# A DiT block: attention probabilities transposed on VectorE and by DMA instead of on TensorE

## The chip, the cores and the metric

One Trainium2 chip, one of its cores. The time is the device time of one execution in microseconds; a kernel is run several times and the median is compared. One further execution is taken with the hardware profiler, and its trace gives every instruction of the five engines: PE (TensorE), DVE (VectorE), ACT (ScalarE), POOL (GpSimd) and SP (SyncE, which here only issues DMAs).

## The reference, cut to what matters

B = 2 batches of N = 256 tokens, D = 1152, two heads of 576, F = 4608, all bf16.

```python
mod = (_silu(c) @ w_mod).reshape(B, 6, 1, D)
shift_a, scale_a, gate_a, shift_m, scale_m, gate_m = [mod[:, i] for i in range(6)]
h = _layernorm(x) * (1 + scale_a) + shift_a
q, k, v = split(h @ wqkv)                                  # 2 heads of 576
attn = _softmax(einsum('bqhd,bkhd->bhqk', q, k) * 576 ** -0.5)
a = einsum('bhqk,bkhd->bqhd', attn, v).reshape(B, N, D) @ wo
x = x + gate_a * a
h2 = _layernorm(x) * (1 + scale_m) + shift_m
return x + gate_m * (_gelu(h2 @ w_fc1) @ w_fc2)
```

## The kernel before

The 512 tokens are four tiles of 128 (t = 0 to 3; batch b holds tiles 2b and 2b + 1). The program is written as a list of units, each for one engine. A small planner (`Sched`) works out what each unit must wait for from the bytes that it reads and writes, and fixes the order on every engine before the program is emitted. TensorE and SyncE keep the order in which the units are written. VectorE, ScalarE and GpSimd are ordered by a list schedule with assumed costs. Each engine works through its order strictly, so a unit that waits holds up all units behind it on its engine. A DMA has a semaphore of its own (60 of them are reused in turn), and SyncE issues a DMA only when the buffer and the data are ready.

The stretch around the change, in the order of TensorE:

1. `q_kt*`, `proj`: the projections to q, the last with `proj(WQ, 8)`, beside which `S_b_h` computes the scores of batch b and head h (index idx = 2b + h) into one PSUM bank each (`s_bank`).
2. `s_and_softmax`: VectorE takes the row maxima (`smax`, L1005), scales them (`snb`, L1006), ScalarE takes exponentials with row sums (`sexp`, L1009), VectorE takes reciprocals (`sri`, L1011) and multiplies (`spn`, L1013). The result `PP[idx]` has queries on partitions.
3. `pt_transposes`: four 128x128 TensorE transposes for each idx (L695, helper `tr`) turn P so that keys lie on partitions; a copy (`PT_ev`) moves the result from PSUM to `PTS[idx]`, on VectorE for batch 0 and on ScalarE for batch 1.
4. `v_proj(t, ci)`: twelve tiles of nine matmuls of width 384 (L692, helper `mm`), three PSUM banks in turn, copied out by ScalarE (`v_ev`). The transposes stand between these tiles.
5. `rows`: the rows shift_m and scale_m, 9 x 2 rounds of four matmuls of width 288 that run side by side in four column strips of the array ("quads"). They stand before the last three v tiles. VectorE turns the result (`mt_0`, `mt_1`, L1050).
6. `pv_halves`, `pv`: P V, with `PTS` as the moving operand of width 256; `pv_halves` uses two column strips. VectorE and ScalarE copy the results to `OT`.
7. `wo_tile(t)`: three tiles of nine matmuls of width 384, four PSUM banks in turn (`acc`). VectorE multiplies by the gate (`wo_t1`, L1165), GpSimd adds x (`wo_x1`, L1166), then follow layernorm statistics (`bn_ln2`, `aggr`, `veps`, `rstd` on GpSimd, `nmr2`), ScalarE normalises (`xn2`, L1171), and `xn2_T(t)` transposes on TensorE. Then fc1 and fc2.

Beside this VectorE computes the attention gate gate_a (`attn_gate`: 18 steps `ga_b_kt` of 1152 elements, L1061 and L1064, then `ga_T`, `ga_red` and small ones up to `ga_t`, L1082). It is stored to a scratch tensor in HBM (`st_ga0`, `st_ga1`) and loaded back broadcast over 128 partitions as `GA[b]` (`ld_g0`, `ld_g1`). SyncE loads the weights, all in one order: after the parts of w_mod (`ld_modr`) WO, the first two quarters of WFC1 (`wfc1_load`), `GA`, two more of WFC1, `WGM`, and parts of WFC2. WO takes the bytes of the K weights, WFC1 those of the Q and V weights.

Of the kernel before, what the change touches and what calls it, by code (L numbers as in the profile page):

```python
# [9 lines left out]
SEM_LAT = 120.0  # L10
# [161 lines left out]
class Sched:  # L172
    def __init__(self):
        self.units = []
        self.instrs = []
        self.sb_recs = {}
        self.sb_buckets = defaultdict(set)
        self.bank_pe = defaultdict(list)
        self.bank_other = defaultdict(list)
        self.bank_prev_other = defaultdict(list)  # L180
        self.cur_unit = None
        self.first = {}

    def unit(self, eng, dur, name="", dma_bytes=0, boost=0.0, lat=0.0):
# [20 lines left out]

    def order_after(self, u, prev):
# [74 lines left out]
    def schedule(self, dma_bw=385.0, dma_issue=650.0, dma_lat0=900.0, dma_lat1=600.0, verbose=False):  # L281
# [30 lines left out]
        avail_time = {}  # L312
# [13 lines left out]
        while scheduled < n:  # L326
# [39 lines left out]
            for f, uid in fin_now:  # L366
                for s in units[uid].succ:
                    ndeps[s.uid] -= 1
                    at = max(avail_time.get(s.uid, 0.0), f + (SEM_LAT if True else 0.0))
# [166 lines left out]
def c_dve_tt16(n):  # L536
    return 100.0 + 1.15 * n
# [6 lines left out]
def build_kernel(nc, x, c, wqkv, wo, w_mod, w_fc1, w_fc2, out):  # L544
# [5 lines left out]
    with (  # L550
# [64 lines left out]
        PP = [sb(O_P + i * 1024, 1024).rearrange("p (j k) -> p j k", j=2) for i in range(4)]  # L615
        PTS = [sb(O_PT + i * 1024, 1024).rearrange("p (j k) -> p j k", j=2) for i in range(4)]
        GA = [sb(O_GA + b * 2304, 2304) for b in range(2)]
# [375 lines left out]
        def s_and_softmax(b, h):  # L993
# [17 lines left out]
            dve(165, lambda e: e.reciprocal(out=ri, in_=rsum), [rsum], [ri], "sri_%d" % idx)  # L1011
            rib = ri.unsqueeze(2).broadcast_to([P, 2, 256])
            u = dve(c_dve_tt16(512), lambda e: e.tensor_tensor(out=pp, in0=pp, in1=rib, op=ALU.mult), [pp, ri], [pp], "spn_%d" % idx)  # L1013
            if idx % 2 == 1:
                S.order_after(ga_units[(1, 7) if idx == 1 else (0, 8)], u)

        def pt_transposes(b, h):
            idx = b * 2 + h
            bank = s_bank[(b, h)]
            S.unit("pe", 4 * c_mm(128), "PT_%d_%d" % (b, h))  # L1020
            for kjt in range(2):
                for jq in range(2):
                    tr(ps16(bank, kjt * 256 + jq * 128, 128), PP[idx][:, jq, kjt * 128:(kjt + 1) * 128], IDENT)
            copy_on("dve" if b == 0 else "act", PTS[idx].rearrange("p j k -> p (j k)"), ps16(bank, 0, 512), 512, True, "PT_ev%d" % idx)

        v_banks = [0, 1, 2]
        v_rr = [0]

        def v_proj(t, ci):
            bank = v_banks[v_rr[0] % 3]  # L1030
# [25 lines left out]
        def attn_gate():  # L1056
# [60 lines left out]

        PVB = [(6, 7, 0, 1), (3, 4, 0, 1)]

        def pv_halves():  # L1120
            S.unit("pe", 4 * c_mm(256) + 100.0, "PV_halves")
            for b in range(2):
                for kjt in range(2):
                    for h in range(2):
                        f0 = 512 + 64 * h
                        mm(psum[64 * h:64 * h + 64, 5 * 512 + b * 256:5 * 512 + b * 256 + 256], V[:, 2 * b + kjt, f0:f0 + 64],
                           PTS[b * 2 + h][:, kjt, :], b == 0 and kjt == 0, b == 1 and kjt == 1, skip_group_check=True,
                           tile_position=(0, 64 * h))
# [219 lines left out]
```

## Time and profile before

| | |
|---|---|
| runs, not profiled | 243.26 us median of 3 (242.79 to 243.5) |
| the profiled execution | span 242.5 us from the first to the last instruction; no other time is kept of it |
| granted TensorE clock, mean | 0.993 |
| busy | PE 237.3, DVE 121.5, ACT 67.8, POOL 19.9 us |
| TensorE transposes | 89 in all, 16 of them of P |
| HBM | 50.15 MB read, 212 GB/s over the span |

The span is 0.76 us under the median of the runs. A busy share of PE counts a matmul from its start to its modelled end, and successive matmuls overlap, so the mean duration of a matmul is longer than the distance between two starts; the chain of waits, in which each matmul counts up to the next, is the better measure. The page puts the helper's line on what a helper records, so all matmuls have L692, all transposes by TensorE L695 and all DMA issues L673.

### The profile page before, as it was taken

Reading aid. Unit: us, or ns where it says so; the run is one execution under the profiler, and the core shown is the slowest. Engines: PE = TensorE matmul, PEld = TensorE weight load, DVE = VectorE, ACT = ScalarE, POOL = GpSimd, SP = SyncE. Lnnn points to the kernel's source line nnn. Section 1 sums busy time; section 2 is a strip of 40 time slices with the busy share of each in tenths; the row PEclk is TensorE's granted clock in tenths of the full one; section 3 lists DMA queues with packets and bytes.
Section 4 is the critical chain, followed back from the end, with each engine's and each line's share of the span. In section 5 each row is a group of like instructions: output and inputs, shape, how many; then the busy total and the mean of one; then the engine's idle time right before and its main releaser. Section 6 shows DMA issues by size and latency. Waiting matters only on the chain.

```text
span 242.5 us, 3957 instructions
## 1 busy us (share of the span) xinstructions
PE 237.3 (98%) x1699; PEld 145.4 (60%) x1699; DVE 121.5 (50%) x229; ACT 67.8 (28%) x136; POOL 19.9 (8%) x36
## 2 busy tenths in 40 slices
PE   6899999999999999999999999999999999999995
PEld 2688844466666666898544444444666566566564
DVE  2654379988996689669999700000022222111112
ACT  4921440435524206973233322222000000000000
POOL 1300000000002276400000110000000000000000
PEclk9979999999999999999999999999999999999999
DMA  6999999999992999999963499100000000000000
GB/s 221 378 370 392 389 392 390 398 413 402 391 352 79 312 374 391 391 348 398 352 198 83 157 313 374 43 0 3 0 16 19 16 16 16 19 16 16 21 27 20
DMA packets 30363, 51.58 MB, mean 213 GB/s; under 512 B 1547, under 2 KB 15755, under 8 KB 30347
## 3 DMA queue, kind: packets, MB, share of 16 engines
q1 hardware_dynamic: 29888, 50.73, 58.9%
q0 software_dynamic: 288, 0.60, 0.8%
q8 instruction: 13, 0.21, 0.4%
q10 hardware_dynamic: 171, 0.01, 0.0%
q14 instruction: 3, 0.02, 0.0%
HBM read 50.15 MB, written 1.19 MB: 212 GB/s over the span
## 4 chain that ended last, share of the span: by engine, by line
PE 95%; DMA 3%; SPq 1%; DVE 0%; issue 0%
PE psum L692 93%; DMA arena<-in_wqkv_dram 3%; PE psum L695 2%; SPq L673 1%; DVE arena L1290 0%; DVE arena L1291 0%
## 5 line engine op out<-in xcount | busy, mean ns | idle before, releaser
L692 PE MATMUL psum<-arena 128*128 128x384 bf16 (+8 forms) x1610 | 234.0, 314 | 2.4 <-POOL arena L718 1.5
L692 PEld LDWEIGHTS psum<-arena 128*128 128x128 bf16 (+2 forms) x1610 | 139.7, 97 | 92.4 <-issue 3.8
L1290 DVE TENSOR_TENSOR arena<-psum,arena 128x384 f32<-128x384 f32 (+2 forms) x13 | 6.8, 526 | 88.6 <-PE psum L692 88.6
L1200 ACT ACTIVATE arena<-psum 128x512 bf16<-128x512 f32 (+1 forms) x45 | 22.8, 512 | 42.1 <-PE psum L692 42.1
L687 ACT ACTIVATE arena<-psum 128x512 bf16<-128x512 f32 (+6 forms) x34 | 18.2, 560 | 37.9 <-PE psum L692 37.9
L1064 DVE SCALAR_TENSOR_TENSOR arena<-arena 128x1152 f32<-128x1152 bf16 x16 | 21.9, 1408 | 0.0
L1095 DVE SCALAR_TENSOR_TENSOR arena<-arena 128x1152 f32<-128x1152 bf16 x16 | 21.4, 1414 | 0.0
L1166 POOL TENSOR_TENSOR arena<-arena 128x384 f32<-128x384 f32 x12 | 10.9, 912 | 11.7 <-DVE arena L1165 9.5
L740 DVE BATCH_NORM_STATS2 arena<-arena 128x6 f32<-128x384 f32 (+1 forms) x18 | 9.5, 549 | 3.8 <-DMA arena<-in_x_dram 3.8
L673 POOL DMA_DIRECT2D dit_scratch<-arena x4 | 2.4, 609 | 96.6 <-DVE arena L1082 60.3
L689 DVE CAST arena<-psum 128x512 bf16<-128x512 f32 x11 | 7.2, 687 | 5.3 <-PE psum L692 5.3
L1165 DVE TENSOR_TENSOR arena<-psum,arena 128x384 f32<-128x384 f32 x12 | 6.7, 556 | 3.7 <-PE psum L692 3.7
L1171 ACT ACTIVATE arena<-arena 128x1152 bf16<-128x1152 f32 x4 | 5.4, 1344 | 9.8 <-DVE arena L1170 9.8
L695 PE MATMUL psum<-arena 128*128 128x128 bf16 (+1 forms) x89 | 7.4, 225 | 0.4 <-DMA arena<-in_c_dram 0.4
L695 PEld LDWEIGHTS psum<-arena 128*128 128x128 bf16 (+1 forms) x89 | 6.3, 102 | 2.2 <-DMA arena<-in_c_dram 1.1
L1291 DVE TENSOR_TENSOR arena<-arena 128x384 bf16<-128x384 f32 (+2 forms) x13 | 6.9, 527 | 0.5
L1190 ACT ACTIVATE arena<-psum,arena 128x128 bf16<-128x128 bf16 x16 | 6.1, 455 | 3.0 <-PE psum L695 2.2
L1187 DVE TENSOR_SCALAR arena<-psum,arena 128x128 bf16<-128x128 bf16 x20 | 5.5, 336 | 2.9 <-PE psum L695 2.9
L1009 ACT ACTIVATE arena<-psum,arena 128x256 bf16<-128x256 f32 x8 | 3.7, 471 | 0.2 <-DVE arena L1006 0.2
L744 POOL TENSOR_TENSOR arena<-arena 128x1 f32<-128x1 f32 x6 | 3.3, 555 | 4.7 <-DVE arena L743 4.5
L1005 DVE TENSOR_REDUCE arena<-psum 128x2 f32<-128x512 f32 x4 | 2.8, 688 | 0.9 <-PE psum L692 0.7
L962 ACT ACTIVATE arena<-arena 128x256 bf16<-128x256 bf16 x6 | 2.5, 495 | 1.5 <-DVE arena L956 1.5
(60 smaller groups left out, 53.9 us busy)
## 6 DMA issues: line engine op xcount, KB each, us to landing
arena<-in_w_fc_dram SPq DMA_DIRECT2D x9, 1152.0 KB, 8.0
arena<-in_w_fc_dram SPq DMA_DIRECT2D x4, 2592.0 KB, 17.6
arena<-in_wqkv_dram SPq DMA_DIRECT2D x18, 288.0 KB, 9.3
arena<-in_w_mod_dram SPq DMA_DIRECT2D x6, 864.0 KB, 12.3
arena<-in_w_mod_dram SPq DMA_DIRECT2D x3, 1728.0 KB, 20.5
arena<-in_wqkv_dram SPq DMA_DIRECT2D x1, 2592.0 KB, 17.6
arena<-in_wo_dram SPq DMA_DIRECT2D x1, 2592.0 KB, 24.9
arena<-in_w_mod_dram SPq DMA_DIRECT2D x1, 2592.0 KB, 18.5
```

The lines of the kernel that those rows point to most:

```text
L687: act(c_act(n), lambda e: e.activation(out=dst, in_=src, func=ACTF.Copy), [src], [dst], name)
L689: return dve(c_dve_psum16(n) if psum16 else c_dve_psum32(n), lambda e: e.tensor_copy(dst, src), [src], [dst], name)
L692: S.instr(lambda e: e.matmul(o, lhsT=l, rhs=r, start=st, stop=sp, **kw), reads=[l, r], writes=[o])
L695: S.instr(lambda e: e.transpose(o, i_, idn), reads=[i_, idn], writes=[o])
L740: dve(550, lambda e, s=s, o=o: e.bn_stats(out=o, in_=s), [s], [o], "bn_%s_%d" % (tag, ci))
L1064: ga_units[(b, kt)] = dve(150 + FG * 1.1, lambda e, o=o, w=w, s1=s1: e.scalar_tensor_tensor(out=o, in0=w, scalar=s1, in1=o, op0=ALU.mult, ...
L1095: u = dve(1300, lambda e, o=o, w=w, s1=s1: e.scalar_tensor_tensor(out=o, in0=w, scalar=s1, in1=o, op0=ALU.mult, op1=ALU.add), [w, s1, o], ...
L1165: dve(550, lambda e, o=o, ga=ga, x1c=x1c: e.tensor_tensor(out=x1c, in0=o, in1=ga, op=ALU.mult), [o, ga], [x1c], "wo_t1_%d_%d" % (t, ci))
L1166: S.op("pool", 930, lambda e, xs=xs, x1c=x1c: e.tensor_tensor(out=x1c, in0=x1c, in1=xs, op=ALU.add), reads=[x1c, xs], writes=[x1c], name=" ...
L1200: act(c_act(ntok), lambda e: e.activation(out=dst, in_=o, func=ACTF.Gelu_apprx_tanh), [o], [dst], "gelu_%d_%d" % (f, tok0))
L1290: dve(c_dve_psum32(w), lambda e, o=o, gm=gm, t1=t1: e.tensor_tensor(out=t1, in0=o, in1=gm, op=ALU.mult), [o, gm], [t1], "fc2_t1_%d_%d" % ( ...
L1291: dve(c_dve_32(w), lambda e, t1=t1, x1c=x1c, ost=ost: e.tensor_tensor(out=ost, in0=t1, in1=x1c, op=ALU.add), [t1, x1c], [ost], "fc2_out_%d ...
```

## The change

- The softmax keeps its exponentials in `PP[idx]`, and ScalarE scales them by the reciprocals, in two halves (`spn_idx_jq`), in place of VectorE's multiplication.
- VectorE turns P in blocks of 32x32 in one instruction for each idx (`PT_turn`), reading every fourth key column for each block and writing to the buffers that held `PTS` (now `PTF`). Four DMAs for each idx, issued by SyncE (`mv_pt`), carry rows of 1024 bytes on 32 partitions to 256 bytes on 128 partitions, back into the bytes of `PP`. `PTS[idx]` is now a view of these bytes, in which 256 query columns are eight pieces of 32. No TensorE transposes and no PSUM copies of P remain.
- `rows` moves behind the last v tile, so that `rows`, `pv_halves` and `pv` follow each other. The v tiles use four PSUM banks instead of three; `PVB` and `acc` are rearranged; `OT_ev_4` moves from VectorE to ScalarE.
- The store of the gate moves from GpSimd's queue to SyncE's (`gate_store`).
- SyncE's order becomes: w_mod parts, sixteen moves, WO, WFC1 part 0, the gate's store, `GA`, WFC1 part 1, then as before. WO was issued ahead of the softmax until now.
- `in_order` fixes the order of VectorE, ScalarE and GpSimd around these places by lists of names (without waits), and 66 DMA semaphores are in turn instead of 60.

```diff
-        dma(WO, wo_v, D * D * 2, "ld_wo", run=2304)
...
-            rib = ri.unsqueeze(2).broadcast_to([P, 2, 256])
-            u = dve(c_dve_tt16(512), lambda e: e.tensor_tensor(out=pp, in0=pp, in1=rib, op=ALU.mult), [pp, ri], [pp], "spn_%d" % idx)
...
-        def pt_transposes(b, h):
...
+            for jq in range(2):
+                o, aa = pp[:, jq, :], ri[:, jq:jq + 1]
+                act(c_act(256, 1), lambda e, o=o, aa=aa: e.activation(out=o, in_=o, func=ACTF.Copy, scale=aa), [o, aa], [o], "spn_%d_%d" % (idx, jq))
+            src, flat = pp.rearrange("p j (t x c) -> p c (j t) x", t=2, c=4), PTF[idx]
+            dve(c_dve_32(512), lambda e: e.transpose(flat, src), [src], [flat], "PT_turn%d" % idx)
+            for a in range(4):
+                dma(PPF[idx][:, 128 * a:128 * a + 128], flat[32 * a:32 * a + 32, :], P * 256, "mv_pt%d_%d" % (idx, a), run=256)
...
+        PTS = [f.rearrange("p (a j t i) -> p t j a i", a=4, j=2, t=2) for f in PPF]
...
-        v_banks = [0, 1, 2]
+        v_banks = [7, 0, 1, 2]
...
+        def gate_store():
-            dma(lin[0:64].rearrange("(j p) c -> p j c", j=2), GTA[:, 0:64].rearrange("p (j c) -> p j c", j=2), 4096, "st_ga0", eng="pool")
-            dma(lin[64:72], GTA[0:8, 64:96], 512, "st_ga1", eng="pool")
+            dma(lin[0:64].rearrange("(j p) c -> p j c", j=2), GTA[:, 0:64].rearrange("p (j c) -> p j c", j=2), 4096, "st_ga0")
+            dma(lin[64:72], GTA[0:8, 64:96], 512, "st_ga1")
...
-        PVB = [(6, 7, 0, 1), (3, 4, 0, 1)]
+        PVB = [(6, 7, 0, 1), (2, 5, 6, 7)]
...
-            S.order_after(copy_on("dve", OT[:, 4, :], ps32(5), 512, False, "OT_ev_4"), last_mt[0])
+            copy_on("act", OT[:, 4, :], ps32(5), 512, False, "OT_ev_4")
...
-        acc = [2, 3, 4, 5]
+        acc = [3, 4, 5, 2]
...
         s_and_softmax(1, 1)
-        v_proj(0, 2)
-        pt_transposes(0, 0)
-        v_proj(1, 0)
-        pt_transposes(1, 0)
-        v_proj(1, 1)
-        v_proj(1, 2)
-        pt_transposes(0, 1)
-        v_proj(2, 0)
-        v_proj(2, 1)
-        pt_transposes(1, 1)
-        v_proj(2, 2)
-        rows()
+        dma(WO, wo_v, D * D * 2, "ld_wo", run=2304)
         wfc1_load(0)
-        wfc1_load(1)
+        gate_store()
         for b in range(2):
             dma(GA[b], scratch[0, b].partition_broadcast(P), P * D * 2, "ld_g%d" % b, run=2304)
-        v_proj(3, 0)
-        v_proj(3, 1)
-        v_proj(3, 2)
+        wfc1_load(1)
+        v_proj(0, 2)
+        for t in range(1, 4):
+            for ci in range(NCH):
+                v_proj(t, ci)
+        rows()
         wfc1_load(2)
         wfc1_load(3)
...
+        ga = ["ga_%d_%d" % (b, kt) for kt in range(KT) for b in range(2)]
+        S.in_order("dve", ga)
+        S.in_order("dve", ga[9:10] + ["smax_0", "snb_0"] + ga[10:11] + ["sri_0"] + ga[11:12] + ["smax_2", "snb_2", "PT_turn0", "smax_1", "snb_1", "sri_2"]
+                   + ga[12:13] + ["smax_3", "snb_3", "sri_1", "PT_turn2"] + ga[13:14] + ["PT_turn1", "sri_3"] + ga[14:15] + ["PT_turn3"] + ga[15:16])
+        S.in_order("act", ["sexp_0_0", "sexp_0_1", "qk_ev8", "spn_0_0", "spn_0_1", "v_ev0_0", "sexp_2_0", "sexp_2_1", "sexp_1_0", "sexp_1_1", "v_ev0_1",
+                           "spn_2_0", "spn_2_1", "spn_1_0", "spn_1_1", "v_ev0_2", "sexp_3_0", "sexp_3_1", "v_ev1_0", "spn_3_0", "spn_3_1", "v_ev1_1", "v_ev1_2"])
+        S.in_order("dve", ["ga_t", "mt_0", "mt_1", "OT_ev0_2", "OT_ev0_7", "OT_ev1_2", "OT_ev1_7"])
+        S.in_order("act", ["OT_ev_4", "OT_ev0_0", "OT_ev0_5", "OT_ev1_0", "OT_ev1_5"])
...
+        S.in_order("dve", ["wo_t1_0_0", "wo_t1_0_1", "bn_ln2_0_0", "wo_t1_0_2", "bn_ln2_0_1", "wo_t1_1_0", "bn_ln2_0_2", "aggr_ln2_0", "veps_ln2_0", "wo_t1_1_1", "nmr2_0",
...
```

More of the change, by code (lines that the diff above doesn't have):

```diff
@@ L182, in __init__ @@
         self.first = {}
+        self.loose = set()
     def unit(self, eng, dur, name="", dma_bytes=0, boost=0.0, lat=0.0):
@@ L204, in instr, with in_order @@
         return ins
+    def in_order(self, eng, names):
+        by_name = {u.name: u for u in self.units if u.eng == eng}
+        for a, b in zip(names, names[1:]):
+            if by_name[a] not in by_name[b].deps:
+                by_name[b].deps.add(by_name[a])
+                self.loose.add((by_name[a].uid, by_name[b].uid))
     def order_after(self, u, prev):
@@ L368, in schedule @@
                     ndeps[s.uid] -= 1
-                    at = max(avail_time.get(s.uid, 0.0), f + (SEM_LAT if True else 0.0))
+                    at = max(avail_time.get(s.uid, 0.0), f + (0.0 if (uid, s.uid) in self.loose else SEM_LAT))
                     avail_time[s.uid] = at
@@ L615, in build_kernel @@
         PP = [sb(O_P + i * 1024, 1024).rearrange("p (j k) -> p j k", j=2) for i in range(4)]
-        PTS = [sb(O_PT + i * 1024, 1024).rearrange("p (j k) -> p j k", j=2) for i in range(4)]
+        PPF = [sb(O_P + i * 1024, 1024) for i in range(4)]
+        PTF = [sb(O_PT + i * 1024, 1024) for i in range(4)]
+        PTS = [f.rearrange("p (a j t i) -> p t j a i", a=4, j=2, t=2) for f in PPF]
         GA = [sb(O_GA + b * 2304, 2304) for b in range(2)]
@@ L1011, in s_and_softmax @@
             dve(165, lambda e: e.reciprocal(out=ri, in_=rsum), [rsum], [ri], "sri_%d" % idx)
-            rib = ri.unsqueeze(2).broadcast_to([P, 2, 256])
-            u = dve(c_dve_tt16(512), lambda e: e.tensor_tensor(out=pp, in0=pp, in1=rib, op=ALU.mult), [pp, ri], [pp], "spn_%d" % idx)
-            if idx % 2 == 1:
-                S.order_after(ga_units[(1, 7) if idx == 1 else (0, 8)], u)
-        def pt_transposes(b, h):
[L1018 to L1024, printed above, removed]
-        v_banks = [0, 1, 2]
+            for jq in range(2):
[6 more added lines that the diff above has]
+        v_banks = [7, 0, 1, 2]
         v_rr = [0]
         def v_proj(t, ci):
-            bank = v_banks[v_rr[0] % 3]
+            bank = v_banks[v_rr[0] % 4]
             v_rr[0] += 1
@@ L1126, in pv_halves @@
                         mm(psum[64 * h:64 * h + 64, 5 * 512 + b * 256:5 * 512 + b * 256 + 256], V[:, 2 * b + kjt, f0:f0 + 64],
-                           PTS[b * 2 + h][:, kjt, :], b == 0 and kjt == 0, b == 1 and kjt == 1, skip_group_check=True,
+                           PTS[b * 2 + h][:, kjt], b == 0 and kjt == 0, b == 1 and kjt == 1, skip_group_check=True,
                            tile_position=(0, 64 * h))
-            S.order_after(copy_on("dve", OT[:, 4, :], ps32(5), 512, False, "OT_ev_4"), last_mt[0])
+            copy_on("act", OT[:, 4, :], ps32(5), 512, False, "OT_ev_4")
         def pv(b, h):
@@ L1137, in pv @@
                 for kjt in range(2):
-                    mm(ps32(bank, half * 256, 256), V[:, 2 * b + kjt, g * 128:(g + 1) * 128], PTS[idx][:, kjt, :], kjt == 0, kjt == 1)
+                    mm(ps32(bank, half * 256, 256), V[:, 2 * b + kjt, g * 128:(g + 1) * 128], PTS[idx][:, kjt], kjt == 0, kjt == 1)
             tok = slice(b * 256, (b + 1) * 256)
@@ L1294, in build_kernel @@
         S.n_other_dma_sems = 12
+        ga = ["ga_%d_%d" % (b, kt) for kt in range(KT) for b in range(2)]
[6 more added lines that the diff above has]
+        S.in_order("act", ["OT_ev_4", "OT_ev0_0", "OT_ev0_5", "OT_ev1_0", "OT_ev1_5"])
+        S.in_order("pool", ["wo_x1_0_0", "wo_x1_0_1", "wo_x1_0_2", "wo_x1_1_0", "rstd_ln2_0", "wo_x1_1_1", "wo_x1_1_2", "wo_x1_2_0", "rstd_ln2_1", "wo_x1_2_1", "wo_x1_2_2",
+                            "wo_x1_3_0", "rstd_ln2_2", "wo_x1_3_1", "wo_x1_3_2", "rstd_ln2_3"])
+        S.in_order("dve", ["wo_t1_0_0", "wo_t1_0_1", "bn_ln2_0_0", "wo_t1_0_2", "bn_ln2_0_1", "wo_t1_1_0", "bn_ln2_0_2", "aggr_ln2_0", "veps_ln2_0", "wo_t1_1_1", "nmr2_0",
+                           "bn_ln2_1_0", "wo_t1_1_2", "bn_ln2_1_1", "wo_t1_2_0", "bn_ln2_1_2", "aggr_ln2_1", "veps_ln2_1", "wo_t1_2_1", "nmr2_1", "bn_ln2_2_0", "wo_t1_2_2"])
         S.schedule()
@@ L1299, in build_kernel @@
             sems = {e: es.enter_context(nc.semaphore("c_" + e)) for e in ENGINES}
-            dma_sems = [es.enter_context(nc.semaphore("d%d" % i)) for i in range(60)]
+            dma_sems = [es.enter_context(nc.semaphore("d%d" % i)) for i in range(66)]
             S.emit(nc, block, sems, dma_sems)
```

## The prediction

> **What bounds the kernel now.** First the page: engine shares, and the chain of waits that ended last.
>
> ```profile
> PE 237.3 (98%) x1699; PEld 145.4 (60%) x1699; DVE 121.5 (50%) x229; ACT 67.8 (28%) x136; POOL 19.9 (8%) x36
> PE 95%; DMA 3%; SPq 1%; DVE 0%; issue 0%
> ```
>
> TensorE is the chain: 95% of 242.5 us. Next the chain in order of time around the attention (start, us, what). L692 is a matmul, L695 a TensorE transpose.
>
> ```profile
> 59.46 0.22 PE psum L695 x4
> 59.68 1.46 PE psum L692 x9
> 61.15 0.22 PE psum L695 x4
> ...
> 67.44 0.22 PE psum L695 x4
> 67.67 25.59 PE psum L692 x229
> ```
>
> The four groups of P transposes lie on the chain at 0.22 us each, and no other engine's piece stands between them. So TensorE work taken out is time won, and any new TensorE wait is time lost. The groups by line, VectorE and ScalarE, 49 to 76 and 49 to 82 us (count | busy, mean ns | idle before):
>
> ```profile
> L1064 DVE SCALAR_TENSOR_TENSOR arena<-arena 128x1152 f32<-128x1152 bf16 x9 | 12.5, 1408 | 0.0
> L1013 DVE TENSOR_TENSOR arena<-arena 128x512 bf16<-128x512 bf16 x4 | 2.8, 688 | 0.0
> L1070 DVE STREAM_TRANSPOSE arena<-arena 128x1152 f32<-128x1152 f32 x2 | 2.6, 1356 | 0.0
> L689 DVE COPY arena<-psum 128x512 bf16<-128x512 bf16 x2 | 0.8, 420 | 0.2 <-PE psum L695 0.2
> L1009 ACT ACTIVATE arena<-psum,arena 128x256 bf16<-128x256 f32 x8 | 3.7, 471 | 0.2 <-DVE arena L1006 0.2
> ```
>
> VectorE has almost no idle time before its instructions, ScalarE little work in all. Last SyncE's issues (timeline; start, us) and the DMA list (KB each, us to landing):
>
> ```profile
> 44.15 2.49 SPq L673 DMA_DIRECT2D arena<-in_wo_dram  x1
> 77.02 0.82 SPq L673 DMA_DIRECT2D arena<-dit_scratch  x2
> ...
> arena<-in_w_fc_dram SPq DMA_DIRECT2D x9, 1152.0 KB, 8.0
> arena<-in_wo_dram SPq DMA_DIRECT2D x1, 2592.0 KB, 24.9
> arena<-dit_scratch SPq DMA_DIRECT2D x2, 288.0 KB, 4.3
> dit_scratch<-arena POOLq DMA_DIRECT2D x2, 4.0 KB, 1.9
> ```
>
> WO, issued at 44.15, lands at 69.1: SyncE's transfers land in order of issue (the trace has 62.3 for the load before, 72.5 for the one behind).
>
> **1. Transposes out of TensorE.** 16 x 55.6 ns (0.22 / 4) = -0.89 us, all on the chain.
>
> **2. Rows next to P V.** The piece of 229 matmuls is 117 of width 384 (162 ns apart by the trace's start times), 18 rounds of row quads (120 ns each), 36 slots of width 256 (109 ns): 19.0 + 2.2 + 3.9 = 25.1 us. It took 25.59, so 0.49 us goes to four changes between full and column-tiled matmuls, 0.12 each. The new order has three (into rows, rows to PV_halves, out). If the middle one is free, two: -0.12 to -0.24. The trace has no change from one tiling straight to another; I take -0.12.
>
> **3. VectorE.** Four normalisations (688 ns) go, four turns of 512 bf16 elements come. The nearest rows are the f32 transposes: 1356 ns for 1152 elements and 2578 for 2304 give 1.06 ns each, so 512 cost 0.68 us. The strided read (every fourth element) is in no row: 0.42 us (the bf16 copy) to 1.37 (twice) for each. At 0.69 VectorE gets as much as it gives, less two P copies (0.84). I walked the pinned order with the trace's start-to-start times (gate step 1.34, maximum 0.61, turn 0.61, small ones 0.1): smax_0 at 50.55, PT_turn0 ends 55.5, PT_turn2 59.6, PT_turn1 61.5, PT_turn3 63.6, ga_t 74.4 (before 74.9). At 1.37, PT_turn3 is at 66 and ga_t at 76.6.
>
> The Trainium skill ("VectorE: DVE Perf Modes", The three transpose paths) speaks against the change: 390 ns for a 128x128 on TensorE, 311 on VectorE, with TensorE advised where PSUM will do. By that page, as an estimate, 16 x 0.39 = 6.2 us leave the chain and the time is 237.0; the rows (55.6 ns in the stream) decide against it.
>
> **4. ScalarE** takes eight scalings (0.47 to 0.50 by the nearest rows, 3.9 us) and OT_ev_4 (0.60), and loses two P copies (0.59 each). It idles 18.6 us before its copies in that stretch. Walked in pinned order, each V copy ends 3 us or more before TensorE wants its bank again (four banks instead of three). Cost 0. Without that cover, each late us is a us.
>
> **5. The 16 moves on SyncE.** Quiet issues of 128 rows take 0.34 to 0.6 us; I take 0.5. Queued behind SyncE's wait for a turn are the later moves, WO, WFC1 and the gate. The first land behind the loads ahead of them (62.3); the last four issue by 65.6 and, at the 1.9 to 2.2 us of quiet transfers, land by about 68. Their data are small: 256-byte packets took 18 to 29 ns in the trace, eight to an engine. PV_halves, which waits for all of them, comes at 74.9. Cost 0; 16 more semaphore waits on TensorE, at 51 ns a wait instruction, lie between 0 and 0.82 us. The trace shows TensorE's wait for the row weights at 66.5, 2.6 us before their matmul: its sequencer runs ahead, so I take 0 and keep 0.82.
>
> **6. WO and WFC1 later.** WO issues at 65.6 instead of 44.15. A quiet load has about 2.2 us besides its transfer (1152 KB: 5.5 us, of which 3.4 transfer), WO's transfer took 6.8: it lands at 74.6. Tile wo_0_0 needs it at 79.92 - 1.0 = 78.9. Slack 4.3 us, cost 0. WFC1 part 0 follows at 78.0, wanted at 97.
>
> **7. Gate over SyncE.** The store leaves POOL's queue (1.9 us to landing) and queues on SyncE behind WFC1 part 0: landed about 78.5. SyncE waits for that, with wfc1 parts 1 to 3 and WGM behind it. GA[0] took 3.6 us from issue (77.0 to 80.6): 82.1. Its reader wo_t1_0_0 could start at 80.6, so it is 1.5 us late. TensorE feels it only at the fifth wo tile, which takes bank 3 back at 78.9 + 4 x 1.46 = 84.75: GA[0] by 84.0 is free. The layernorm chain then still has about 2 us before xn2_T(0). Cost 0, slack 1.9 us.
>
> The Trainium skill ("DMA: Bandwidth & Descriptors", Queues, rings and completion order) says that descriptors of one issuer are consumed in ring order on each DMA engine, and that engines alternate between issuers' rings. By that rule the store has lost its own lane; WO's landing agrees on the order, and the late gate below is that case.
>
> **8. The rest.** The pinned orders of POOL and VectorE put each rstd ahead of one or more additions, so xn2 is ready earlier, not later. The WFC2 loads wait for rows and come some 3 us later; part 4 of WFC1 landed at 117.7 and is used at 129. Cost 0.
>
> **Sum.** -0.89 - 0.12 = -1.0 us on a span of 242.5. The runs' median is 243.26, 0.76 above it, which stays: 242.3.
>
> **Rivals.**
> - *Late gate* (slower). If turns cost 1.37 and issues 0.65, PT_turn3 ends at 66.0, the last move issues by 68.6, and WFC1 part 0 lands at 81.0 instead of 78.0. A store 1.5 us behind it and a GA load of 3.6 then give 86.1: the fifth wo tile stalls 2.1 us, net +1.1, 244.4. With 2 us for the store and 4.9 for the load (as GA[1] took) it is 87.9, net +2.9, 246.2. It decides from GA[0] after 84.0, costs the whole gain from 85.0. For: SyncE's order. Against: 1.9 us slack, so it takes two at once. Chance 0.16.
> - *P V slowed by its strided operand* (32-element pieces): at half speed 36 x 0.109 = +3.9, net +2.9, 246.2. Against: the row quads read pieces of the same size and step at four per 120 ns. Chance 0.04; other slow outcomes 0.05.
> - *The gain is eaten.* The 0.82 us of waits, or half a microsecond of lateness at bank 3 or 7: about 243.1, no change by what can be measured, 0.3% or 0.73 us. Chance 0.14.
> - *A transpose is worth its whole duration*, not its place in the stream: the page's group L695 has a mean of 225 ns, 16 of them 3.6 us, less 0.12 more: 239.5. Against: the chain, 0.22 us for four. Chance 0.01.
> - *Forecast*: chance 0.60.
>
> **Numbers.** Faster 0.61, same 0.14, slower 0.25. The forecast case alone spans 241.9 (free middle change, and 0.3 of the runs' spread of 242.79 to 243.5) to 242.6. The range reaches up to the milder late gate: 241.9 to 244.4.
>
> **What would show it.** Right: 73 L695 transposes instead of 89, no group of four on the chain; wo_0_0 about 1.0 us earlier (78.9); TensorE without idle time after 15 us; wo_t1_0_0 starting near 82 on a DMA. Wrong: a TensorE wait after 72 us, named by the moves (step 5), WO (6) or L1165 at bank 3 (7); turns over 0.7 us (3); P V matmuls more than 109 ns apart; four tiling changes' worth of time still there (2).

## The result, and the profile after

The changed kernel takes 246.88 us (median of 4 runs, 246.13 to 247.41) beside 243.18 us (median of 4, 242.79 to 243.5) for the kernel before on the same chip: a ratio of 1.0152, with a 95% interval of 1.0126 to 1.0178. It is 3.7 us slower, where 1.0 us faster was forecast, and lies outside the range. Ratios here and below leave out single executions more than 1.5% above the fastest of the same kernel; the numbers of runs include them.

The page of the kernel after: engines, then the chain that ended last.

```profile
PE 237.2 (97%) x1683; PEld 144.3 (59%) x1683; DVE 121.4 (49%) x226; ACT 70.3 (29%) x143; POOL 18.9 (8%) x34
PE 75%; DVE 12%; DMA 7%; ACT 2%; POOL 2%; SPq 1%; issue 1%; DVEq 0%; POOLq 0%
```

TensorE has the 16 instructions fewer, but its share of the chain has fallen from 95% to 75%, with VectorE and DMA in its place. The chain of waits of the kernel after in order of time (start, us, what) says where. L1084 is `ga_t`, L1169 is `wo_t1`, L1170 is `wo_x1`, L754 is `rstd`, L1174 is `nmr2`, L1175 is `xn2`; L702 and L705 are now the matmul and the TensorE transpose.

```profile
74.27 0.28 DVE arena L1084
74.56 7.03 DMA dit_scratch<-arena
81.61 3.79 DMA arena<-dit_scratch
85.49 0.57 DVE arena L1169
86.20 0.92 POOL arena L1170
...
90.29 0.56 POOL arena L754
90.87 0.98 DVE arena L1174
...
102.26 0.87 DVE arena L1174
103.16 1.35 ACT arena L1175
...
```

The groups of P transposes are gone, as they should be. But the store of the gate is on the chain with 7.03 us (a median of 1.9 us to landing before), the load behind it with 3.79, and from there the chain runs through VectorE and GpSimd up to the layernorm transposes. The waits of TensorE (engine, line, waited for: us in total, times, longest), all but those of the start:

```profile
PE psum L705 <- ACT arena L1175: 2.3, 3, 0.8
PE psum L702 <- DVE arena L1169: 1.0, 1, 1.0
```

The page counts idle time from the modelled end of a matmul. By the distance between starts, less the usual one, the four stalls are 1.16 us up to 86.11 (the fifth wo tile, which takes bank 3 back), and 0.92, 0.88 and 0.95 us ahead of `xn2_T(1)`, `xn2_T(2)` and `xn2_T(3)`: 3.91 us.

SyncE's timeline of the kernel after (start, us) shows what stood ahead of the gate:

```profile
55.78 11.71 SPq L683 DMA_DIRECT2D arena<-arena  x16
67.54 0.59 SPq L683 DMA_DIRECT2D arena<-in_wo_dram  x1
68.18 0.60 SPq L683 DMA_DIRECT2D arena<-in_w_fc_dram  x1
74.56 0.75 SPq L683 DMA_DIRECT2D dit_scratch<-arena  x2
81.61 0.82 SPq L683 DMA_DIRECT2D arena<-dit_scratch  x2
```

By the trace WO landed at 76.93, part 0 of WFC1 at 81.43, the store at 81.59, `GA[0]` at 85.40 (80.62 before). The store has 4 KB and came 0.16 us behind the 1152 KB load that was issued ahead of it.

**Stretches.** All kernels below are compared over three stretches, since executions with a granted clock of 0.993 reach the half-head scores later than those at 1.000 (the kernel after at 49.09 and at 47.48 us in its two traces), and this would otherwise hide a microsecond. S is the start of the half-head scores (TensorE's instructions ahead of it are the same in all), wo0 the start of `wo_0_0`, T3 the end of `xn2_T(3)` (the start of its last transpose and 0.056 us, the step from one transpose to the next). "Late" is the landing of `GA[0]` less wo0. From T3 to the end it is 136.14 to 136.19 us in all kernels but two.

| kernel | S to wo0 | wo0 to T3 | S to T3 | late | TensorE stalls in wo0 to T3 |
|---|---|---|---|---|---|
| before | 31.00 | 26.44 | 57.44 | 0.70 | none |
| after | 30.01 | 30.39 | 60.39 | 6.30 | 1.16, 0.92, 0.88, 0.95 |
| after, second run | 30.01 | 30.42 | 60.43 | 6.33 | 1.19, 0.92, 0.88, 0.95 |

The change did win its 1.0 us, ahead of wo0. It lost 3.95 us between there and T3. 2.95 us is what it costs in these stretches. The medians differ by more; what lies between is in the part ahead of S and in the mix of clocks (see the end of the section on the prediction).

### The profile page after: what moved, and what is told of

Read it like the earlier page. It is cut to its first block, busy times and chain, and to the rows that moved or that the text cites. A ratio compares the mean times of both kernels' runs of the same rounds, so it can differ in the third digit from the quotient of the medians.

```text
span 245.7 us, 3952 instructions
## 1 busy us (share of the span) xinstructions
PE 237.2 (97%) x1683; PEld 144.3 (59%) x1683; DVE 121.4 (49%) x226; ACT 70.3 (29%) x143; POOL 18.9 (8%) x34
## 3 DMA queue, kind: packets, MB, share of 16 engines
HBM read 50.15 MB, written 1.19 MB: 209 GB/s over the span
## 4 chain that ended last, share of the span: by engine, by line
PE 75%; DVE 12%; DMA 7%; ACT 2%; POOL 2%; SPq 1%; issue 1%; DVEq 0%; POOLq 0%
PE psum L702 74%; DMA arena<-in_wqkv_dram 3%; DMA dit_scratch<-arena 3%; DVE arena L1066 3%; DVE arena L1169 2%; DMA arena<-dit_scratch 2%; DVE arena L750 1%; POOL arena L1170 1%; SPq L683 1%; DVE arena L1174 1%; ACT arena L1175 1%; DVE arena L1072 1%; PE psum L705 1%; DVE arena L1074 1%; DVE arena L1191 1%
## 5 line engine op out<-in xcount | busy, mean ns | idle before, releaser
L702 PE MATMUL psum<-arena 128*128 128x384 bf16 (+8 forms) x1610 | 233.5, 314 | 3.3 <-POOL arena L728 1.5
L702 PEld LDWEIGHTS psum<-arena 128*128 128x128 bf16 (+2 forms) x1610 | 139.9, 97 | 93.9 <-issue 3.4
L1204 ACT ACTIVATE arena<-psum 128x512 bf16<-128x512 f32 (+1 forms) x45 | 22.6, 512 | 43.1 <-PE psum L702 43.1
L697 ACT ACTIVATE arena<-psum 128x512 bf16<-128x512 f32 (+5 forms) x33 | 17.7, 557 | 31.8 <-PE psum L702 31.8
L1170 POOL TENSOR_TENSOR arena<-arena 128x384 f32<-128x384 f32 x12 | 10.8, 910 | 74.7 <-DVE arena L1169 74.7
L1175 ACT ACTIVATE arena<-arena 128x1152 bf16<-128x1152 f32 x4 | 5.4, 1350 | 14.1 <-DVE arena L1174 14.1
L1169 DVE TENSOR_TENSOR arena<-psum,arena 128x384 f32<-128x384 f32 x12 | 6.4, 538 | 5.5 <-DMA arena<-dit_scratch 5.5
L705 PE MATMUL psum<-arena 128*128 128x128 bf16 (+1 forms) x73 | 5.9, 224 | 2.7 <-ACT arena L1175 2.3
L705 PEld LDWEIGHTS psum<-arena 128*128 128x128 bf16 (+1 forms) x73 | 4.8, 102 | 4.9 <-ACT arena L1175 3.2
L1191 DVE TENSOR_SCALAR arena<-psum,arena 128x128 bf16<-128x128 bf16 x20 | 5.6, 332 | 3.3 <-PE psum L705 3.3
L1194 ACT ACTIVATE arena<-psum,arena 128x128 bf16<-128x128 bf16 x16 | 6.0, 458 | 1.8 <-PE psum L702 0.9
L683 POOL DMA_DIRECT2D dit_scratch<-arena x2 | 1.3, 652 | 34.7 <-DVE arena L1114 34.7
L754 POOL TENSOR_TENSOR arena<-arena 128x1 f32<-128x1 f32 x6 | 3.3, 550 | 7.9 <-DVE arena L753 7.7
L1022 ACT ACTIVATE arena<-arena 128x256 bf16<-128x256 bf16 x8 | 3.6, 502 | 0.2 <-DVE arena L1019 0.2
```

The source lines that it names most:

```text
L697: act(c_act(n), lambda e: e.activation(out=dst, in_=src, func=ACTF.Copy), [src], [dst], name)
L702: S.instr(lambda e: e.matmul(o, lhsT=l, rhs=r, start=st, stop=sp, **kw), reads=[l, r], writes=[o])
L705: S.instr(lambda e: e.transpose(o, i_, idn), reads=[i_, idn], writes=[o])
L1169: dve(550, lambda e, o=o, ga=ga, x1c=x1c: e.tensor_tensor(out=x1c, in0=o, in1=ga, op=ALU.mult), [o, ga], [x1c], "wo_t1_%d_%d" % (t, ci))
L1170: S.op("pool", 930, lambda e, xs=xs, x1c=x1c: e.tensor_tensor(out=x1c, in0=x1c, in1=xs, op=ALU.add), reads=[x1c, xs], writes=[x1c], name=" ...
L1175: act(1344, lambda e: e.activation(out=xn2, in_=x1, func=ACTF.Identity, scale=rs, bias=nm), [x1, rs, nm], [xn2], "xn2_%d" % t)
```

## Experiments: who made the gate late

Theory: part 0 of WFC1, issued ahead of the store, makes the gate late, and the late gate makes all four stalls. Rivals: SyncE itself, as a queue for the store; WO's later place; the pinned orders on VectorE and GpSimd.

**The gate ahead of part 0 of WFC1.**

```
         dma(WO, wo_v, ..., "ld_wo")
-        wfc1_load(0)
         gate_store()
         for b in range(2): dma(GA[b], ...)
+        wfc1_load(0)
         wfc1_load(1)
```

> The changed kernel with one move: WFC1 part 0 goes behind the two GA loads in SyncE's order (WO, gate store, GA, GA, WFC1 part 0, WFC1 part 1). Theory L (the late gate is the whole loss, and it is late because its store waits behind WFC1 part 0 in SyncE's queue): the store lands close behind WO, about 77.5 us instead of 81.6, GA[0] about 81.2 instead of 85.4, TensorE has no stall after wo tile 0 begins, the span falls by about 4.1 us to 241.5, 1.0 us under the kernel before. Rival T (the turns, the moves or the pinned orders cost TensorE time of their own): some of the four stalls (1.2, 0.9, 0.9, 1.0 us) stay, span 242.5 or more. Rival W (WFC1 part 0, now late, is wanted): a stall at the first fc1 tile.

Measured: 242.48 us (12 runs) beside 242.95 (28 runs); ratio 0.9983, interval 0.9963 to 1.0004. S to wo0 30.01, wo0 to T3 26.44, so S to T3 56.44: 1.00 us less than before, no stall. The timeline of SyncE:

```profile
74.70 0.76 SPq L683 DMA_DIRECT2D dit_scratch<-arena  x2
78.45 0.82 SPq L683 DMA_DIRECT2D arena<-dit_scratch  x2
79.32 9.31 SPq L683 DMA_DIRECT2D arena<-in_w_fc_dram  x4
```

The store is issued at the same time as in the kernel after and lands after 3.7 us instead of 7.0; GA[0] lands at 81.77, 2.53 us late. The page's chain is TensorE's again:

```profile
PE 94%; DMA 3%; SPq 1%; issue 0%; DVE 0%
```

With this one load taken from ahead of the store and the gate's loads, the whole 3.95 us are gone. WO, the moves, the turns, the pinned orders and SyncE as the store's queue are all still in this kernel, and none of them stalls TensorE here. But the time of the gate isn't all that changed. The planner works out its orders anew for every edit, and from `xn2_T(0)` on it gave VectorE and ScalarE other ones: ScalarE now has one copy of `xn2_T(2)` ahead of `xn2` of tile 3, where it had three. The next section shows what that is worth.

**The store on GpSimd's queue again**, part 0 left where it is.

```
-            dma(lin[0:64]..., GTA[:, 0:64]..., 4096, "st_ga0")
-            dma(lin[64:72], GTA[0:8, 64:96], 512, "st_ga1")
+            dma(lin[0:64]..., GTA[:, 0:64]..., 4096, "st_ga0", eng="pool")
+            dma(lin[64:72], GTA[0:8, 64:96], 512, "st_ga1", eng="pool")
```

> The changed kernel with the gate's store back on GpSimd's queue; the GA loads stay behind WFC1 part 0 on SyncE. The store then lands near 76.5 us, SyncE issues GA[0] near 76.7, and GA[0] lands about 1.9 us behind WFC1 part 0 (81.4), at 83.3: about 2 us earlier than in the changed kernel, and inside the limit of 84.0 that the prediction gave. Theory P (lateness costs only from 84.0 on, at the fifth wo tile): no stall, span 241.5. Theory C (the chain of gate, addition and statistics on VectorE and GpSimd cannot catch up under the new orders, so lateness is paid again at xn2_T(1), xn2_T(2) and xn2_T(3)): no stall at the fifth wo tile, but 1 to 2 us at the later transposes, span 242.5 to 243.5.

Measured: 244.31 us (10 runs), ratio 1.0053 (1.0038 to 1.0068). Issued at 73.50, the store landed at 79.32, not at 76.5 as expected: 5.8 us on a queue of its own, while WO (landed 75.83) and part 0 (80.29) were moving. The own queue saves about 1.2 us and no more; the 1.9 us of before is the price beside idle DMA engines (2% busy from 75.6 to 77.0 there, 90% here). GA[0] is 4.99 us late, and TensorE has these waits in the stretch:

```profile
PE psum L705 <- ACT arena L1175: 0.6, 1, 0.6
PE psum L702 <- DVE arena L1191: 0.5, 1, 0.5
```

There is none at bank 3 (no L1169), since 4.99 is within the 5.1 us that the prediction allowed (84.0 less 78.9). Yet wo0 to T3 is 28.30, 1.86 us too long: by the starts 0.74 ahead of `xn2_T(1)` and 1.10 in the first fc1 tile, which waits for VectorE's copies of the transposes (L1191). The prediction's limit holds for bank 3 and not for the chain behind it. VectorE and ScalarE have the planner's order of the kernel with the gate first.

**WO early, as before**, the rest as after: `dma(WO, ...)` stands again behind the last K projection.

```
         proj(WK, 8, 17, HK, 7)
+        dma(WO, wo_v, D * D * 2, "ld_wo", run=2304)
...
-        dma(WO, wo_v, D * D * 2, "ld_wo", run=2304)
         wfc1_load(0)
```

> The changed kernel with the WO load back at its old place ahead of the softmax. WO lands near 70 us; the sixteen moves queue behind it and land near 70 as well, 5 us before P V wants them; WFC1 part 0, issued near 67.6, lands near 74; the store near 76.4; GA[0] near 80.0. Theory L: no TensorE stall, span 241.5, as when GA goes ahead of WFC1 part 0. Rival M (the moves are late behind WO): TensorE stalls at the half-head P V near 75 us, by as much as the moves land after that.

Measured: 243.02 us (12 runs), ratio 1.0009 (0.9985 to 1.0033). GA[0] is 3.23 us late, wo0 to T3 26.58 with one stall of 0.13. Part 0, issued at 70.74, lands at 76.61, so the store behind it lands at 77.96. WO's new place is thus the other half of the cause: in the kernel after the two loads keep the DMA engines 82% busy from 67.5 to 81.4, which is when the gate has to pass. The planner's order is again that of the kernel with the gate first. The moves landed as late as 72.3 here, behind WO, and still no P V matmul waited. Its stretch from S to T3 is 0.85 us under before's, and yet the median is even; its trace reaches S at 48.15, and why it doesn't gain there is open.

**The store on SyncE alone**, in the kernel before (its WO, loads and orders unchanged).

```
+        def gate_store():
-            dma(lin[0:64]..., 4096, "st_ga0", eng="pool")
-            dma(lin[64:72], ..., 512, "st_ga1", eng="pool")
+            dma(lin[0:64]..., 4096, "st_ga0")
+            dma(lin[64:72], ..., 512, "st_ga1")
...
         wfc1_load(1)
+        gate_store()
```

> The kernel before with the gate's store moved from GpSimd's queue to SyncE's, behind WFC1 parts 0 and 1, and nothing else. WFC1 part 1 has landed at 75.6 us in the kernel before, so the queue is nearly empty when the store is issued at 74.9: the store lands near 77, GA[0] near 80.6. Theory L (only what stands ahead in the queue makes the store late): no stall, same time as before within 0.2 us. Rival (a store on SyncE's queue is slow or holds up the loads behind it by itself): GA[0] after 82 us, a stall at the fifth wo tile or later, 0.5 us or more slower.

Measured: 244.16 us (4 runs), ratio 1.0044 (1.003 to 1.0058). The store landed at 75.89 and GA[0] at 79.69, before its reader could start at 80.29. Part 1 of WFC1, ahead of it in the queue, landed at 75.72, and the store 0.17 us behind that: SyncE as such delays the gate little when the loads ahead are nearly through. The 0.80 us stall ahead of `xn2_T(0)` has another cause, the planner's order. On GpSimd it put `rstd` of tile 0 behind six additions instead of five, done at 89.67; on VectorE it put `nmr2_0` behind eight of the multiplications by the gate instead of six, and the eighth waits for TensorE's tile, so `nmr2_0` ran at 91.00 and `xn2_0` ended at 92.54. The tail from T3 is 136.52, 0.37 us longer than elsewhere, all of it behind TensorE's last matmul, where the last instruction comes 0.8 us behind the landing of the last output store instead of under 0.5; why is open.

## Experiments: why a late gate costs more than bank 3

TensorE loses 1.16 us at bank 3 and 2.75 us at the three transposes. `nmr2` multiplies two 128x1 columns. VectorE's timeline in the kernel after (start, us, what, count) has it with

```profile
90.87 0.98 DVE L1174 SCALAR_TENSOR_TENSOR arena<-arena 128x1 f32<-128x1 f32 x1 [0.20 <-POOL arena L754]
95.48 0.86 DVE L1174 SCALAR_TENSOR_TENSOR arena<-arena 128x1 f32<-128x1 f32 x1
102.26 0.86 DVE L1174 SCALAR_TENSOR_TENSOR arena<-arena 128x1 f32<-128x1 f32 x1 [0.19 <-POOL arena L754]
```

and the fourth, with GpSimd idle, takes 0.15. GpSimd's timeline there:

```profile
90.93 0.90 POOL L1170 TENSOR_TENSOR arena<-arena 128x384 f32<-128x384 f32 x1
...
94.89 0.55 POOL L754 TENSOR_TENSOR arena<-arena 128x1 f32<-128x1 f32 x1 [0.21 <-DVE arena L753]
95.41 0.91 POOL L1170 TENSOR_TENSOR arena<-arena 128x384 f32<-128x384 f32 x1
```

The instruction of 128 numbers ends at 91.85, 0.02 us after the addition of 90.93 (91.83); the next at 96.34, after the addition of 95.41 (96.32). The pinned order sets an addition right behind each `rstd`, and `nmr2` waits for that `rstd`, so it always starts with an addition when additions are queued. The Trainium skill ("SBUF — State Buffer", SBUF: two separate sides) describes it: VectorE with two SBUF inputs and a GpSimd instruction that reads SBUF need one pair of ports, as a lock, for the whole instruction. The ends above agree. In the first pair `nmr2` is recorded 0.06 us ahead of the addition (90.87 and 90.93) and is held all the same.

**`nmr2` with one tensor input**, the kernel after otherwise unchanged.

```
-  e.scalar_tensor_tensor(out=nm, in0=m, scalar=-1.0, in1=rs, op0=ALU.mult, op1=ALU.mult)
+  e.tensor_scalar(out=nm, in0=m, scalar1=rs, scalar2=-1.0, op0=ALU.mult, op1=ALU.mult)
```

> The changed kernel, gate as late as ever, with nmr2 (one value for each partition) as an instruction with one SBUF tensor and a pointer scalar instead of two SBUF tensors. In the changed kernel three of the four nmr2 take 0.98, 0.86 and 0.86 us and end with the GpSimd addition that runs beside them; the fourth, with GpSimd idle, takes 0.15. Theory S (VectorE is held while GpSimd runs, because this form wants what GpSimd holds; VectorE is the chain while it catches up, so the 2.25 us are paid in full at the later stalls): nmr2 takes about 0.15 each, the three later stalls fall from 2.75 us to about 0.7, the span by about 2 us. Rival H (this form is held as well): nmr2 stays near 0.9 and the time stays. Rival G (GpSimd's additions are the chain, not VectorE): nmr2 gets short and the stalls stay above 2 us.

Measured: 244.24 us (5 runs) beside 243.13 (15 runs), ratio 1.0054 (1.0039 to 1.0068). VectorE's timeline of this kernel:

```profile
89.09 0.21 DVE L1174 TENSOR_SCALAR arena<-arena 128x1 f32<-128x1 f32 x1 [0.20 <-POOL arena L754]
92.94 0.21 DVE L1174 TENSOR_SCALAR arena<-arena 128x1 f32<-128x1 f32 x1
```

It isn't held: 0.20 to 0.22 us in all four. wo0 to T3 falls from 30.39 to 28.01 with GA[0] 5.74 us late; stalls of 0.59 at bank 3 and 0.95 ahead of `xn2_T(3)` remain. So of the 2.75 us at the transposes 1.80 was the hold, together with the late gate; another 0.57 went at bank 3, which is the 0.56 us by which the gate came earlier. TensorE goes on from bank 3 0.71 us behind the gate's landing in both kernels, so the earlier gate doesn't shorten the stalls behind it.

**The 0.95 us ahead of `xn2_T(3)`** is neither the gate nor the hold. The chain of the kernel after goes there (L1204 is a gelu of fc1, L1194 ScalarE's copy of a transpose out of PSUM):

```profile
104.56 0.68 PE psum L705 x9
...
106.25 0.38 ACT arena L1204
106.64 1.04 ACT arena L1194 x3
107.68 1.24 ACT arena L1175
...
108.97 0.68 PE psum L705 x9
```

It starts at TensorE and comes back to it: in the planner's order ScalarE has a gelu and three copies of `xn2_T(2)` ahead of `xn2` of tile 3, so `xn2_T(3)` begins 4.41 us behind `xn2_T(2)`, whenever that was. It is 4.41 in every kernel with three copies there (after, its second run, this one, and one below whose gate is in time), and 3.45 or 3.46 in all others. The kernel with the gate first has one copy there. So of the 3.95 us that it won, 0.95 came from the planner's new order.

**The two pinned orders taken out** of the kernel after.

```
-        S.in_order("pool", ["wo_x1_0_0", "wo_x1_0_1", "wo_x1_0_2", "wo_x1_1_0", "rstd_ln2_0", ...])
-        S.in_order("dve", ["wo_t1_0_0", "wo_t1_0_1", "bn_ln2_0_0", ..., "nmr2_0", ...])
```

> The changed kernel without the two hand-written orders of the wo stage (GpSimd's wo_x1 and rstd, VectorE's wo_t1, bn_ln2 and nmr2); the planner orders them as in the kernel before. The gate stays as late as in the changed kernel (GA[0] near 85.4). Theory O (the pinned orders make VectorE wait for GpSimd while it catches up, and so cause the three later stalls of 0.9 us): the later stalls shrink to under 1.5 us in all from 2.75, span 244.5 or less. Rival (lateness alone does it, in either order): the four stalls stay within 0.5 us in sum, span about 245.7.

Measured: 244.78 us (7 runs), ratio 1.0077 (1.0049 to 1.0104). GA[0] is 5.84 us late, and there are stalls of 0.70 at bank 3 and 1.27 ahead of `xn2_T(0)`, none later: wo0 to T3 28.42. Without the pins the first chain is slower, and the later ones, with `nmr2` at 0.86, 0.53, 0.16 and 0.16, catch up. So this order is the cheaper one with a late gate; but of the 1.48 us less at the transposes 0.95 are ScalarE's copies, which the planner has placed behind `xn2` of tile 3 here.

**The pinned orders on top of the store on SyncE alone**, to see whether they heal its 0.80 us.

```
+        S.in_order("pool", ["wo_x1_0_0", ...])
+        S.in_order("dve", ["wo_t1_0_0", ...])
```

> The kernel before with the gate's store on SyncE, as in the run that came out 1 us slower, and with the two pinned orders of the wo stage. There GA[0] landed at 79.7, before its reader could start (80.3), and the one stall of 0.80 us at xn2_T(0) followed the planner's new order, which put rstd of tile 0 on GpSimd behind six additions instead of five. Theory: the order, not the store, made that stall; with rstd of tile 0 behind four additions it goes, and the distance from the half-head scores to the end of xn2_T(3) is 57.44 us again. Rival: the store on SyncE costs by itself, and 0.5 us or more stay.

Measured: 244.7 us (4 runs) beside 242.86 (23 runs), ratio 1.0071 (1.0048 to 1.0093). The stall ahead of `xn2_T(0)` is gone, but 0.40 and 0.95 ahead of `xn2_T(2)` and `xn2_T(3)` have come, so it is no faster: S to T3 is 58.82, not the 57.44 expected. The 0.95 are ScalarE's three copies again, with a gate that landed at 79.28, before its reader could start at 80.27. For the 0.40 VectorE's timeline names the place; L1196 copies a layernorm transpose of tile 0 out of PSUM:

```profile
92.47 0.60 DVE L1196 TENSOR_SCALAR arena<-psum,arena 128x128 bf16<-128x128 bf16 x2 [1.24 <-PE psum L703]
92.98 0.15 DVE L1179 SCALAR_TENSOR_TENSOR arena<-arena 128x1 f32<-128x1 f32 x1
...
99.19 0.86 DVE L1179 SCALAR_TENSOR_TENSOR arena<-arena 128x1 f32<-128x1 f32 x1 [0.19 <-POOL arena L752]
```

VectorE idles 1.24 us for TensorE, with `nmr2_1` queued behind those copies, and `nmr2_2` is held. The pins name only some of the instructions; the planner fits the others in between, differently in each kernel. The tail is 136.52 here too.

## Experiments: what is won when the gate is in time

**The gate first, and `nmr2` with one input**: both edits above together.

> The changed kernel with both cures: WFC1 part 0 behind the GA loads, and nmr2 with one SBUF tensor. With the gate on time TensorE had no stall even with the long nmr2, so theory L and theory S expect nothing more from the second cure: from the half-head scores to the end of xn2_T(3) 56.44 us as with the first cure alone, 0.7 to 1.0 us faster than before in time, and nmr2 at about 0.21 us each. If it is faster than 56.3, nmr2 had a cost with the gate on time too.

Measured: 242.48 us (12 runs) beside 242.86 (23), ratio 0.9985 (0.997 to 1.0). S to T3 56.44, GA[0] 3.06 us late, no stall.

**The gate first, and no pinned orders.**

> The changed kernel with WFC1 part 0 behind the GA loads, without the two pinned orders of the wo stage. GA[0] lands 2.5 us after wo tile 0 begins, as in the version with the pinned orders, which has no stall. If the pinned orders only hurt (theory O taken further), no stall here either: 56.44 us from the half-head scores to the end of xn2_T(3). Rival: the kernel before had 0.28 us between the end of xn2 of tile 1 and xn2_T(1), and the planner puts rstd of tile 0 and 1 behind one more addition; a gate 1.8 us later than before then costs 0.3 to 1.5 us at xn2_T(0) or xn2_T(1), and the pinned orders are what makes a moderately late gate free.

Measured: 242.68 us (10 runs), ratio 0.9985 (0.9968 to 1.0001). S to T3 56.44, 2.90 us late, no stall. With the gate in time neither the pins nor the form of `nmr2` matter in these kernels: a hold that ends before TensorE asks costs nothing. None of them has three copies ahead of `xn2` of tile 3.

**Rows next to P V alone**, in the kernel before.

```
-        PVB = [(6, 7, 0, 1), (3, 4, 0, 1)]
+        PVB = [(6, 7, 0, 1), (2, 5, 6, 7)]
...
-         acc = [2, 3, 4, 5]
+         acc = [3, 4, 5, 2]
...
-         rows()
          ...
          v_proj(3, 2)
+         rows()
```

`OT_ev_4` goes to ScalarE here as in the change.

> The kernel before with the rows moved next to P V and the PSUM banks and the copy of OT_ev_4 that this needs; TensorE transposes, loads and gate as before. By the prediction's step 2 it gains 0.12 us (three changes of tiling instead of four), 0.24 if the change from four column strips to two costs nothing. From the half-head scores to the end of xn2_T(3): 57.44 - 0.12 = 57.3 us, where the changed kernel with its gate on time took 56.44. The rest, 0.89, is then the transposes'. If it comes out at 57.4 or more, step 2 gave nothing or the stalls that it brings ate it.

Measured: 242.68 us (11 runs) beside 243.13 (15), ratio 0.9984 (0.9969 to 0.9998). S to T3 57.33: 0.11 us less, no stall.

**The kernel before and the kernel after once more**, unchanged, for the table of stretches.

> The kernel before, unchanged, once more with a profile on the chip of these runs. Its first profile has a granted clock of 0.993 and a span of 242.5; the runs beside the other experiments have spans near 241.2 at clock 1.000. Expected: span near 241.2, the half-head scores starting about 1.3 us earlier than 48.9, and from there to the end of xn2_T(3) 57.4 us as in the first profile. If that last distance differs by more than 0.1 us, the comparisons of the stretch by this distance are not sound.

> The changed kernel, unchanged, once more, to have its trace on the chip of these runs. Its first profile is at clock 0.993, those of most experiments at 1.000. Expected: GA[0] about 5.8 us after wo tile 0 begins instead of 6.3 where the clock is 1.000 (TensorE then reaches wo earlier, but so do the turns), the same four stalls, 60.2 to 60.5 us from the half-head scores to the end of xn2_T(3) (60.39 in its first profile), 1.3 to 1.8% slower than before.

Before: one run, again at a clock of 0.993 and not the 1.000 expected; 31.01, 26.44, 57.44, the same to 0.01 us. After: 246.18 us (4 runs), ratio 1.0131 (1.0106 to 1.0156), with the same four stalls; the gate is 6.33 us late at a clock of 1.000 too, where 5.8 was expected.

The kernels in order of lateness, and what wo0 to T3 has over 26.44:

| kernel | late | over 26.44 | of it bank 3 | of it ScalarE's copies |
|---|---|---|---|---|
| before | 0.70 | 0 | 0 | 0 |
| rows alone | 0.76 | 0 | 0 | 0 |
| gate first | 2.53 | 0 | 0 | 0 |
| gate first, no pins | 2.90 | 0 | 0 | 0 |
| gate first, new `nmr2` | 3.06 | 0 | 0 | 0 |
| WO early | 3.23 | 0.14 | 0 | 0 |
| store on GpSimd | 4.99 | 1.86 | 0 | 0 |
| after, new `nmr2` | 5.74 | 1.57 | 0.59 | 0.95 |
| after, no pins | 5.84 | 1.98 | 0.70 | 0 |
| after | 6.30 | 3.95 | 1.16 | 0.95 |

The two kernels with the store on SyncE alone are left out: their gate was in time, and what they lose comes from the planner's order. The others don't all have one order either, so the rows show more than lateness. The loss from lateness begins somewhere above 3 us (0.14 at 3.23, nothing measured from there to 4.99), bank 3 only near 5.1. The 3.95 us of the kernel after are thus 1.16 at bank 3 for the late gate, 1.80 for the late gate and the hold together, and 0.95 for ScalarE's order; 0.04 are left over.

## Why the prediction was wrong

**Steps 1 and 2 (transposes, rows) were right and right in size.** Forecast -0.89 and -0.12; measured -0.99 to wo0 for both, -0.11 for the rows alone, so -0.88 for the transposes by subtraction. Sixteen transposes are worth their place in the stream, 0.9 us, not their mean duration. The 0.39 us each that the prediction cites from the Trainium skill ("VectorE: DVE Perf Modes", The three transpose paths) isn't what they are worth in this stream.

**Steps 3 and 4 were right.** VectorE's turns in the kernel after:

```profile
L1024 DVE STREAM_TRANSPOSE arena<-arena 128x512 bf16<-128x512 bf16 x4 | 2.8, 706 | 0.0
```

A turn takes 0.71 us (0.69 taken), so the strided read costs next to nothing here, `PT_turn3` ends at 63.7 (63.6), `ga_t` at 74.5 (74.4). ScalarE's scalings take 0.50 us, and no V bank came late. P V's strided operand streams at 109 ns a matmul, as before.

**Step 5: the term was mis-sized.** The step looked for a wait of TensorE on the moves, and there was none: their data landed by 68.8 (about 68), and 16 more waits on TensorE cost nothing. But what the moves take of SyncE delays all that is queued behind them. An issue takes 0.60 us, one every 0.645, not 0.5. From `PT_turn2` on, SyncE has 12 of them in a row: 59.9 + 12 x 0.645 = 67.6, and WO goes out at 67.5 instead of 65.6. The range of 0.34 to 0.6 stood in the prediction; its upper end was the answer, and the middle was taken.

**Step 6: in time, yet it set the trap.** WO landed at 76.93 (74.6) for a use at 79.10. Part 0 of WFC1 came 4.5 us behind it, not 3.4 (4.46 with the store on GpSimd's queue too, so it isn't the store; why is open).

**Step 7 failed.** GA[0] at 85.40, forecast 82.1. The 3.3 us are: 1.9 from SyncE's issues, 0.4 from WO's own load, 1.1 from part 0, less 0.3 because the store came 0.16 us behind part 0 instead of 0.5, and 0.2 from the load of GA. Slack was 1.9 us, and the slow issue alone used it up, since it moves everything behind it on the same queue. The prediction said that it took two mishaps at once and gave the late gate 0.16; with the issue at 0.645 any further one was enough. The rule cited there from the Trainium skill ("DMA: Bandwidth & Descriptors", Queues, rings and completion order), that descriptors of one issuer are consumed in ring order, agrees with the store's landing 0.16 us behind part 0. The other half of it, that the engines alternate between issuers' rings, gave little here: the store on GpSimd's queue still took 5.8 us.

**Its price failed too.** The rival of the late gate put the whole loss at bank 3: 2.1 us for a gate at 86.1. That its dearer case comes out at 246.2, near the measured 246.88, is luck: it has the gate at 87.9. For the measured 85.40 its limit gives 6.30 - 5.1 = 1.2, and 1.16 was measured, so that part was exact. 1.80 of the other 2.75 us come from the sentence "the layernorm chain then still has about 2 us before xn2_T(0)". That was counted for the first tile alone, and right for it: there is no stall ahead of `xn2_T(0)`. `xn2_T(1)` and `xn2_T(2)` follow, and VectorE and GpSimd, late and with `nmr2` held, don't catch up. The last 0.95 belong to step 8.

**Step 8 failed.** The pinned orders were to put each `rstd` ahead of additions, so that `xn2` is ready earlier, at cost 0. But the addition set behind `rstd` holds `nmr2` for 0.98, 0.86 and 0.86 us. The timeline of before showed such a hold already:

```profile
89.84 0.62 DVE L1170 SCALAR_TENSOR_TENSOR arena<-arena 128x1 f32<-128x1 f32 x1
```

The next `nmr2` takes 0.55 there, the other two 0.16; the prediction didn't look at the shortest instructions' durations. And `xn2` of tile 3 came later, not earlier: the step counted the pinned instructions alone, and the planner set ScalarE's three copies, which no pin names, ahead of it (0.95 us).

**The base.** "0.76 us outside the span" joined a profiled execution at a granted clock of 0.993 to a median of executions mostly at 1.000. Where span and time are of the same run, they differ by 1.7 to 1.8 us in every kernel. The forecast difference doesn't hang on it.

**The best version** is the change with the gate ahead of part 0: 242.48 us. Its stretch from S to T3 is 1.00 us shorter than before's, but its median only 0.5 us (ratio 0.9983, interval up to 1.0004): not told from no change. At a granted clock of 1.000 alone it is 242.24 (9 runs) beside 242.95 (26 runs), 0.7 us. The 0.3 us left over lie ahead of S by subtraction, and the kernel after has them too: at 1.000 it is 246.18 (4 runs) beside 242.86 (22 runs), 3.32 us for 2.99 in the stretches. Why is open: the kernel before has no trace at 1.000, and those of the other kernels at 1.000 reach S at 47.48 to 48.15, so single traces scatter by more than this.

## To carry to other kernels

When a small transfer on which work hangs is moved to another queue, list the loads issued ahead of it with their landing times, and treat every error in the issue times of that queue as one error that shifts all of them. Then price lateness at each later consumer of the chain, not just at the first buffer that runs out. Where a planner orders the engines, compare its orders before and after an edit, ahead of giving the edit the credit or the blame. And look at the shortest instructions: one whose durations scatter fourfold is being held by somebody, and the cure may be another form of it.

## What the runs showed of the hardware

- VectorE's instruction of two 128x1 SBUF columns takes 0.15 us with GpSimd idle, up to 0.99 beside GpSimd's 384-wide addition, and then ends 0.02 us after it. With one column as the scalar operand it takes 0.20 to 0.22 and isn't held.
- The store of the gate (4 KB) took a median of 1.9 us beside idle DMA engines, 3.7 us behind the rest of WO, 5.8 us on GpSimd's own queue beside two loads, and 7.0 us behind both on SyncE.
- An SBUF to SBUF move over 128 partitions costs SyncE 0.60 us, one each 0.645 us; the sixteen took 11.7 us of it, with one wait of 1.4 us among them.
- P V's moving operand in pieces of 32 elements streamed as fast as the contiguous one of before (109 ns for 256 columns).
